# The RMS norm's work between two MLPs taken from two queues instead of one

## The chip, the cores and the metric

The kernel runs on one core of a Trainium2 chip. The metric is the device time of one execution in microseconds (us). The engines are named as the profile names them: PE (TensorE matmul) and PEld (its weight loads), DVE (VectorE), ACT (ScalarE), POOL (GpSimd), SP (SyncE, which here issues DMAs).

## The reference

Attention over 2 x 8 heads of 768 tokens with a band of 96 tokens, 8 global tokens and a linear distance bias, then two MLPs on the 1536 tokens of width 512, with an RMS norm between them:

```
attn_out = _attn_ref(q, k, v, n_global, n_local)
x = attn_out.transpose(0, 2, 1, 3).reshape(B * S, H * D)
h = x @ w_in                                  # 512 -> 2048
x = (h * tanh(log1p(exp(h)))) @ w_out         # 2048 -> 512
rms = sqrt(mean(x * x, axis=-1, keepdims=True) + 1e-06)
xn = x / rms * rms_g
g, val = xn @ w_gate, xn @ w_val              # 512 -> 1536 each
out = (g * sigmoid(g) * val) @ w_out2         # 1536 -> 512
```

All inputs and the output are float32.

## The kernel before

Every product is made of three matmuls: both factors are held as a high part, rounded to the matmul's type, and a low part, the rest (high x high, high x low, low x high). The weights arrive as float32 bits and are turned into the two parts on the way: a `Piece` is one 128 x 512 tile of weights, whose integer steps (L154 to L175) and low part (L194) run on DVE and whose high part runs on ACT (L190). The 1536 tokens stand in four blocks of 384 tokens.

The kernel has three stages, attention, the first MLP (`mlp1`, `mish1`) and the second (`mlp2`). The first MLP has 32 steps, eight to each quarter of the 2048 hidden columns: in step s PE makes the products of two chunks of 128 hidden columns for one block (`products`, L362, 24 matmuls of 384 columns) and then, through `flush`, the accumulation of the step before (`accumulate`, L414, 18 matmuls of 512 columns, into the three PSUM banks s0 to s2). ACT and DVE turn the products into the activation: tanh, arctan and sine on ACT (L382, L387, L388, with a load of ACT's table ahead of tanh and of arctan), a multiplication on DVE (L391), the high part on ACT (L488), the low part on DVE (L492). At the end of a step the next weight piece is begun (`begin`), two in every eighth step. After every second accumulation DVE adds the banks to the block's sums (L426). The second MLP has 48 steps of one chunk: 24 matmuls for gate and value, nine for the accumulation of the step before.

Between the two stands the norm of each block (`rms_norm`), which is queued when the block's last accumulation is recorded. It has three parts. `inverse`: three squares with a sum along the row on ACT (L459, whose unwanted output goes to PSUM bank s3), then two small instructions on POOL (L464, L467). `scale`: three multiplications of the sums on DVE (L471). `split_y`, four times: three transposes on PE into bank s3 (L442), a copy with the norm's gain on ACT that makes the high part (L446) and a subtraction on DVE that makes the low part (L447). The four results of a block are what its products in the second MLP read.

The order of the work on each engine is the order in which the program records it; there is no scheduler. The norm's parts stand in one list, `deferred`, five entries to a block: the inverse, the scaling with the first split, and three more splits. `do_deferred` takes one entry: once at the end of a step of the first MLP, and in a step of the second MLP once between the products and the accumulation and once behind the accumulation. A block's first step in the second MLP empties the list as far as it needs.

Of the kernel before, what the change touches and what calls it, by code (L numbers as in the profile page):

```python
# [22 lines left out]
NK = DM // P  # L23
# [27 lines left out]
def tile_attention_mish_swiglu(  # L51
# [31 lines left out]
    def nm(s):  # L83
        uid[0] += 1
        return f"{s}_{uid[0]}"

    def bank(tag, bufs=1):
        return psum.tile([P, BANK], F32, tag=tag, bufs=bufs, name=nm(tag))

    def mm_bank():  # L90
        return bank("mm", 4)
# [9 lines left out]
    order = []  # L101
# [20 lines left out]
    def conv_alloc(i):  # L122
        wpool = wearly if i % sum(SLOTS) < SLOTS[0] else late[0]
        W[order[i]] = wpool.tile([P, 2, WPIECE], F32R, tag="w", name=nm("w"))
# [212 lines left out]
    def fresh():  # L337

        for x in (W, staged, ys):
            x.clear()  # L340
        for x in (begun, pend, deferred, acc):
            del x[:]
        loaded[0], started[0] = 0, NW_EARLY
        for i in range(NW_EARLY):
            conv_alloc(i)
        for blk in range(NBLK):
            xs[blk] = [
                hl.tile([P, 2, BT], F32R, tag="hl", name=nm("hl")) for _ in range(NK)
            ]
# [7 lines left out]
    def products(ps, wkey, c, xs, kcs=tuple(range(NK))):  # L357
        col = slice((c % 4) * P, (c % 4 + 1) * P)
        for kc in kcs:
            w = W[wkey, kc, c // 4]  # L360
            for i, (wi, xi) in enumerate(((0, 0), (0, 1), (1, 0))):
                pe.matmul(  # L362
                    ps[:, 0:BT],
                    w[:, wi, col],
                    xs[kc][:, xi, :],
                    start=kc == 0 and i == 0,
                    stop=kc == NK - 1 and i == 2,
                )
# [25 lines left out]
    started = [NW_EARLY]  # L394
    begun = []

    def begin(n):
        for _ in range(n):
            begun.append(Piece(started[0]))
            begun[-1]("b3")  # L400
            started[0] += 1
# [4 lines left out]
    def accumulate(wkey, gt, c, blk, done):  # L406

        w = W[wkey, c]
        if c % 4 == 0:
            acc[:] = [bank(f"s{m}") for m in range(TB)]  # L410
        for m in range(TB):
            tok = slice(m * P, (m + 1) * P)
            for i, (gi, wi) in enumerate(((0, 0), (0, 1), (1, 0))):
                pe.matmul(  # L414
                    acc[m],
                    gt[:, gi, tok],
                    w[:, wi, :],
                    start=c % 4 == 0 and i == 0,
                    stop=c % 4 == 3 and i == 2,
                )  # L420
            if c % 4 == 3:
                if c == 3:
                    dve.tensor_copy(sums[blk][:, m, :], acc[m])
                else:
                    y = sums[blk][:, m, :]
                    dve.tensor_tensor(y, y, acc[m], op=ALU.add)  # L426
                done(m)

    acc = []
    ys = {}  # L430

    deferred = []

    def do_deferred():
        if deferred:
            deferred.pop(0)()

    def split_y(y, blk, kc):
        t = hl.tile([P, 2, BT], F32R, tag="hl", name=nm("hl"))
        tr = bank("s3")  # L440
        for m in range(TB):
            pe.transpose(  # L442
                tr[:, m * P : (m + 1) * P], y[:, m, kc * P : (kc + 1) * P], ident
            )
        g = gcol[:, kc : kc + 1]
        act.activation(t[:, 0, :], tr[:, 0:BT], AF.Copy, scale=g)  # L446
        dve.scalar_tensor_tensor(  # L447
            t[:, 1, :], tr[:, 0:BT], g, t[:, 0, :].bitcast(F32),
            op0=ALU.mult, op1=ALU.subtract,
        )  # L450
        ys.setdefault(blk, []).append(t)

    def rms_norm(blk):
        y = sums[blk]
        ss = cpool.tile([P, 2, TB], F32, tag="ss", name=nm("ss"), bufs=2)

        def square(m):
            junk = bank("s3")
            act.activation(junk, y[:, m, :], AF.Square, accum_out=ss[:, 0, m : m + 1])  # L459

        def inverse():
            for m in range(TB):
                square(m)
            pool.tensor_scalar(  # L464
                ss[:, 1, :], ss[:, 0, :], 1.0 / DM, 1.0e-6, op0=ALU.mult, op1=ALU.add
            )
            pool.tensor_tensor(ss[:, 0, :], ss[:, 1, :], mhalf, op=ALU.pow)  # L467

        def scale():
            for m in range(TB):  # L470
                dve.tensor_scalar(  # L471
                    y[:, m, :], y[:, m, :], ss[:, 0, m : m + 1], None, op0=ALU.mult
                )

        deferred.append(inverse)
        deferred.append(lambda: [scale(), split_y(y, blk, 0)])
        deferred.extend([lambda kc=kc: split_y(y, blk, kc) for kc in range(1, NK)])

    pend = []

    def flush(n):
        while len(pend) > n:
            pend.pop(0)()


    def split_hi(x):
        gt = gp.tile([P, 2, BT], F32R, tag="g", name=nm("g"))
        act.activation(gt[:, 0, :], x, AF.Copy)  # L488
        return gt

    def split_lo(gt, x):
        dve.tensor_tensor(gt[:, 1, :], x, gt[:, 0, :].bitcast(F32), op=ALU.subtract)  # L492

    def chunks(s):
        return [4 * (s // (2 * NBLK)) + 2 * (s % 2) + i for i in range(2)]

    def mish1(s, mish):

        blk, cs = s // 2 % NBLK, chunks(s)
        for i in range(2):  # L500
            mish.tanh(i)
        flush(0)
        mish.cosine()
        old = begun[:]
        del begun[:]
        for piece in old[:1]:
            piece("hi")
        for i in range(2):
            mish.times(i)
        for piece in old[:1]:  # L510
            piece("lo")
        gt = [split_hi(mish.t[:, i, :]) for i in range(2)]
        for piece in old[1:]:
            piece("hi")
        for i in range(2):
            split_lo(gt[i], mish.t[:, i, :])
        for piece in old[1:]:
            piece("lo")
        do_deferred()
        begin(BEGUN1[s])  # L520

        def later():
            def done(m):
                if m == TB - 1 and cs[1] == NC1 - 1:
                    rms_norm(blk)

            for c, g in zip(cs, gt):
                accumulate("out", g, c, blk, done)

        pend.append(later)  # L530

    def mlp1(s0):
        for s in range(s0, NC1 * NBLK // 2):
            banks = [mm_bank() for _ in range(2)]
            for ps, c in zip(banks, chunks(s)):
                products(ps, "in", c, xs[s // 2 % NBLK])
            mish1(s, Mish(banks))

    def mlp2():
        for s in range(NC2 * NBLK):  # L540
            blk = s // 4 % NBLK
            c = 4 * (s // (4 * NBLK)) + s % 4
            pg, pv = mm_bank(), mm_bank()
            if s % 4 == 0:
                while len(ys.get(blk, ())) < NK:
                    do_deferred()
            for kc in range(NK):
                products(pg, "gate", c, ys[blk], (kc,))
                products(pv, "val", c, ys[blk], (kc,))
            do_deferred()  # L550
            flush(0)
            do_deferred()
            r = dpool.tile([P, 2, BT], F32, tag="d", name=nm("r"))[:, 0, :]
            act.activation(r, pg[:, 0:BT], AF.Silu)  # L554
            dve.tensor_tensor(r, r, pv[:, 0:BT], op=ALU.mult)  # L555
            gt = split_hi(r)
            split_lo(gt, r)
            for piece in begun:
                piece.rest()
            del begun[:]  # L560
            begin(BEGUN2[s])

            def later(blk=blk, c=c, gt=gt):
                def done(m):
                    if c == NC2 - 1:
                        row = blk * BT + m * P
                        sp.dma_start(out[row : row + P, :], sums[blk][:, m, :])

                accumulate("out2", gt, c, blk, done)

            pend.append(later)
        flush(0)
        assert started[0] == len(order) and not begun and not deferred

    def mlps(s, mish=None):

# [10 lines left out]

    def attention_banded():
        fresh()
        mm = [mm_bank() for _ in range(4)]  # L590
        with ExitStack() as st:
# [211 lines left out]

    def attention_general():
        fresh()
        mm = [mm_bank() for _ in range(4)]
        with ExitStack() as st:
# [148 lines left out]
```

## Time and profile before

| | |
|---|---|
| median of 3 runs | 701.08 us (700.76 to 701.08) |
| the profiled execution | 700.8 us |
| its span, first to last instruction | 699.0 us |
| mean granted clock of TensorE | 0.989 |
| PE busy | 674.5 us, 96% of the span |
| PEld busy | 589.4 us, 84% |
| DVE, ACT, POOL busy | 451.1, 386.8, 70.2 us |

The attention fills about the first 110 us of the span (its first products of the first MLP are mixed into its end), the first MLP follows to about 371, the second to the end. A matmul's end is modelled, so a group of them is best measured from its start to the start of the next. The granted clock is 1.00 at the higher of PE's two levels, 2.4 GHz, and 0.50 at the lower, 1.2 GHz.

### The profile page before, as it was taken

Reading aid. Unit: us, or ns where it says so; the run is one execution under the profiler, and the core shown is the slowest. Engines: PE = TensorE matmul, PEld = TensorE weight load, DVE = VectorE, ACT = ScalarE, POOL = GpSimd, SP = SyncE. Lnnn points to the kernel's source line nnn. Section 1 sums busy time; section 2 is a strip of 40 time slices with the busy share of each in tenths; the row PEclk is TensorE's granted clock in tenths of the full one; section 3 lists DMA queues with packets and bytes.
Section 4 is the critical chain, followed back from the end, with each engine's and each line's share of the span. In section 5 each row is a group of like instructions: output and inputs, shape, how many; then the busy total and the mean of one; then the engine's idle time right before and its main releaser. Section 6 shows DMA issues by size and latency. Waiting matters only on the chain.

```text
span 699.0 us, 10036 instructions
## 1 busy us (share of the span) xinstructions
PE 674.5 (96%) x3760; PEld 589.4 (84%) x3760; DVE 451.1 (65%) x1067; ACT 386.8 (55%) x722; POOL 70.2 (10%) x128
## 2 busy tenths in 40 slices
PE   8999999999999999999898998999999999999997
PEld 3656668999999999998797886999999999999996
DVE  6787846887788778776885676874367775331332
ACT  5889869888888888888684542222113222111111
POOL 3667740000000000001001000000000000000000
PEclk9999999999999999999999998999999999999999
DMA  7977511231121113221112121131022100010111
GB/s 241 291 237 202 177 62 34 88 91 60 61 92 60 61 61 90 77 76 60 61 61 60 31 60 61 62 108 43 1 61 90 61 31 0 1 46 1 45 46 49
DMA packets 26728, 54.20 MB, mean 78 GB/s; under 512 B 2608, under 2 KB 14640, under 8 KB 26672
## 3 DMA queue, kind: packets, MB, share of 16 engines
q1 hardware_dynamic: 25968, 53.16, 23.9%
q8 instruction: 31, 0.51, 0.3%
q10 hardware_dynamic: 704, 0.33, 0.2%
q14 instruction: 25, 0.20, 0.1%
HBM read 50.34 MB, written 3.15 MB: 77 GB/s over the span
## 4 chain that ended last, share of the span: by engine, by line
PE 81%; DVE 8%; ACT 8%; issue 1%; POOL 1%; DMA 0%; DVEq 0%; SPq 0%; ACTq 0%; POOLq 0%
PE mm L362 43%; PE s L414 31%; PE mm L640 2%; PE s L725 2%; ACT e L671 2%; PE s L705 1%; DVE e L661 1%; ACT s L459 1%; DVE x L426 1%; PE s L442 1%; ACT g L488 1%; DVE hl L447 1%; DVE hl L353 1%; DVE bits L175 1%; ACT hl L352 1%
## 5 line engine op out<-in xcount | busy, mean ns | idle before, releaser
L362 PE MATMUL mm<-hl,w 128*128 128x384 f32 x1920 | 350.9, 337 | 0.0
L362 PEld LDWEIGHTS mm<-hl,w 128*128 128x128 f32 x1920 | 337.2, 188 | 6.7 <-issue 1.0
L414 PE MATMUL s<-w,g 128*128 128x512 f32 x1008 | 248.5, 396 | 0.0
L414 PEld LDWEIGHTS s<-w,g 128*128 128x128 f32 x1008 | 190.2, 190 | 36.8
L554 ACT ACTIVATE r<-mm 128x384 f32<-128x384 f32 x48 | 23.6, 491 | 141.1 <-PE mm L362 141.1
L555 DVE TENSOR_TENSOR r<-r,mm 128x384 f32<-128x384 f32 x48 | 26.4, 550 | 69.2 <-ACT r L554 69.2
L426 DVE TENSOR_TENSOR x<-x,s 128x512 f32<-128x512 f32 x60 | 40.8, 687 | 46.1 <-PE s L414 46.1
L488 ACT ACTIVATE g<-r 128x384 fp32r<-128x384 f32 x48 | 25.2, 526 | 65.6 <-DVE r L555 65.6
L391 DVE TENSOR_TENSOR d<-d,mm 128x384 f32<-128x384 f32 x64 | 32.5, 549 | 40.4 <-ACT d L388 40.4
L690 POOL TENSOR_SCALAR e<-e,s 128x256 f32<-128x256 f32 (+1 forms) x96 | 47.9, 513 | 35.0 <-DVE bias L621 10.2
L671 ACT ACTIVATE e<-e,s 128x256 f32<-128x256 f32 (+1 forms) x96 | 46.1, 481 | 7.9 <-DVE s L661 7.6
L169 DVE SCALAR_TENSOR_TENSOR bits<-stage,bits 128x512 int32<-128x512 int32 x68 | 48.2, 708 | 2.1
L175 DVE SCALAR_TENSOR_TENSOR bits<-stage,bits 128x512 int32<-128x512 int32 x68 | 47.2, 694 | 2.0
L492 DVE TENSOR_TENSOR g<-r,g 128x384 fp32r<-128x384 f32 x48 | 26.8, 558 | 28.4 <-ACT g L488 28.4
L488 ACT ACTIVATE g<-d 128x384 fp32r<-128x384 f32 x64 | 33.5, 526 | 19.3 <-DVE d L391 17.7
L382 ACT ACTIVATE d<-mm 128x384 f32<-128x384 f32 x64 | 30.8, 492 | 20.8 <-PE mm L362 19.2
L386 ACT ACT_TABLE_LOAD x32 | 41.1, 1283 | 0.6
L194 DVE TENSOR_TENSOR w<-bits,w 128x512 fp32r<-128x512 f32 x60 | 41.3, 688 | 0.0
L382 ACT ACT_TABLE_LOAD x31 | 39.8, 1283 | 0.6
L190 ACT ACTIVATE w<-bits 128x512 fp32r<-128x512 f32 x60 | 37.0, 616 | 0.0
L640 PE MATMUL mm<-k,q 64*128 64x256 f32 (+1 forms) x168 | 31.9, 410 | 4.5 <-DVE s L661 2.6
L661 DVE CUSTOM_DVE_ANT_0 e<-mm,bias 128x256 f32<-128x256 f32 (+1 forms) x96 | 35.0, 396 | 0.6 <-POOL e L690 0.6
(82 smaller groups left out, 510.4 us busy)
## 6 DMA issues: line engine op xcount, KB each, us to landing
stage<-in_w_out_dram SPq DMA_DIRECT2D x28, 512.0 KB, 3.2
stage<-in_w_in_dram SPq DMA_DIRECT2D x16, 512.0 KB, 3.9
stage<-in_w_gate_dram SPq DMA_DIRECT2D x12, 512.0 KB, 3.4
stage<-in_w_val_dram SPq DMA_DIRECT2D x12, 512.0 KB, 3.5
k<-in_kT_dram SPq DMA_DIRECT2D x7, 704.0 KB, 4.2
out_dram<-x SPq DMA_DIRECT2D x12, 256.0 KB, 2.1
q<-in_qT_dram SPq DMA_DIRECT2D x7, 384.0 KB, 5.1
v<-in_v_dram SPq DMA_DIRECT2D x7, 384.0 KB, 6.2
```

The source lines that it names most:

```text
L169: dve.scalar_tensor_tensor(self.bits, self.lw, 29, self.bits, op0=ALU.logical_shift_right, op1=ALU.bitwise_or,)
L175: dve.scalar_tensor_tensor(self.bits, self.hw, -1073741824, self.bits, op0=ALU.bitwise_and, op1=ALU.bitwise_or,)
L194: engine.tensor_tensor(self.wt[:, 1, :], self.fl, self.wt[:, 0, :].bitcast(F32), op=ALU.subtract)
L362: pe.matmul(ps[:, 0:BT], w[:, wi, col], xs[kc][:, xi, :], start=kc == 0 and i == 0, stop=kc == NK - 1 and i == 2,)
L382: act.activation(self.t[:, i, :], self.h[i], AF.Tanh, scale=0.5)
L414: pe.matmul(acc[m], gt[:, gi, tok], w[:, wi, :], start=c % 4 == 0 and i == 0, stop=c % 4 == 3 and i == 2,)
L426: dve.tensor_tensor(y, y, acc[m], op=ALU.add)
L488: act.activation(gt[:, 0, :], x, AF.Copy)
L640: pe.matmul(banks[j][:, 0 : n * P], qs[b, p][r, t * P : (t + 1) * P], ks[b, p][r, 0, :] if t == 0 else ks[b, p][r, t : t + NT : NT - 1, :] ...
L661: dve.tensor_tensor_reduce(e[:, j, 0:n], banks[j][:, 0:n], bias0[:, h, :] if t == 0 else bias[:, h, :], scale=-0.125, scalar=3.0e38, op0=A ...
L671: act.activation(e[:, j, 0:n], e[:, j, 0:n], AF.Exp, scale=-1.0, bias=s[:, 0, j : j + 1], accum_out=s[:, 1, j : j + 1],)
L690: pool.tensor_scalar(e[:, j, 0:n], e[:, j, 0:n], s[:, 3, j : j + 1], 0.0, op0=ALU.mult, op1=ALU.add,)
```

## The change

The list `deferred` becomes two. `ends` holds the inverse and the scaling of each block; one entry is taken at the end of a step, in both MLPs. `between` holds the four splits; they are put there when the scaling is recorded, and one is taken in a step of either MLP between the products and the accumulation. In the first MLP that place is behind the tanh, ahead of `flush`. A step of the second MLP thus records one split where it recorded up to two, and a block's scaling and its first split are no longer in one entry.

```diff
@@ -338,7 +338,7 @@
 
         for x in (W, staged, ys):
             x.clear()
-        for x in (begun, pend, deferred, acc):
+        for x in (begun, pend, between, ends, acc):
             del x[:]
         loaded[0], started[0] = 0, NW_EARLY
         for i in range(NW_EARLY):
@@ -429,11 +429,12 @@
     acc = []
     ys = {}
 
-    deferred = []
-
-    def do_deferred():
-        if deferred:
-            deferred.pop(0)()
+
+    between, ends = [], []
+
+    def do_one(work):
+        if work:
+            work.pop(0)()
 
     def split_y(y, blk, kc):
         t = hl.tile([P, 2, BT], F32R, tag="hl", name=nm("hl"))
@@ -471,10 +472,9 @@
                 dve.tensor_scalar(
                     y[:, m, :], y[:, m, :], ss[:, 0, m : m + 1], None, op0=ALU.mult
                 )
-
-        deferred.append(inverse)
-        deferred.append(lambda: [scale(), split_y(y, blk, 0)])
-        deferred.extend([lambda kc=kc: split_y(y, blk, kc) for kc in range(1, NK)])
+            between.extend([lambda kc=kc: split_y(y, blk, kc) for kc in range(NK)])
+
+        ends.extend([inverse, scale])
 
     pend = []
 
@@ -499,6 +499,7 @@
         blk, cs = s // 2 % NBLK, chunks(s)
         for i in range(2):
             mish.tanh(i)
+        do_one(between)
         flush(0)
         mish.cosine()
         old = begun[:]
@@ -516,7 +517,7 @@
             split_lo(gt[i], mish.t[:, i, :])
         for piece in old[1:]:
             piece("lo")
-        do_deferred()
+        do_one(ends)
         begin(BEGUN1[s])
 
         def later():
@@ -541,15 +542,12 @@
             blk = s // 4 % NBLK
             c = 4 * (s // (4 * NBLK)) + s % 4
             pg, pv = mm_bank(), mm_bank()
-            if s % 4 == 0:
-                while len(ys.get(blk, ())) < NK:
-                    do_deferred()
+            assert len(ys[blk]) == NK
             for kc in range(NK):
                 products(pg, "gate", c, ys[blk], (kc,))
                 products(pv, "val", c, ys[blk], (kc,))
-            do_deferred()
+            do_one(between)
             flush(0)
-            do_deferred()
             r = dpool.tile([P, 2, BT], F32, tag="d", name=nm("r"))[:, 0, :]
             act.activation(r, pg[:, 0:BT], AF.Silu)
             dve.tensor_tensor(r, r, pv[:, 0:BT], op=ALU.mult)
@@ -557,6 +555,7 @@
             split_lo(gt, r)
             for piece in begun:
                 piece.rest()
+            do_one(ends)
             del begun[:]
             begin(BEGUN2[s])
 
@@ -570,7 +569,7 @@
 
             pend.append(later)
         flush(0)
-        assert started[0] == len(order) and not begun and not deferred
+        assert started[0] == len(order) and not begun and not between and not ends
 
     def mlps(s, mish=None):
 
```

PE, around the step in which the first block's first set of transposes stands (`ident,x`; mm is a bank of products, s an accumulation or bank s3). Before:

```order
L414 MATMUL s_561_3545<-w_3052,g_3495 128x512 x3
L414 MATMUL s_562_3546<-w_3052,g_3495 128x512 x3
L442 MATMUL s_567_3583<-ident,x_84 128x128 [waits DVE_49,PE_49,Activation_49]
L442 MATMUL s_567_3583<-ident,x_84 128x128 [waits DVE_49] x2
L362 MATMUL mm_3605<-hl_182,w_2684 128x384 x3
L362 MATMUL mm_3605<-hl_183,w_2756 128x384 x3
```

Now:

```order
L362 MATMUL mm_3599<-hl_184,w_2828 128x384 x3
L362 MATMUL mm_3599<-hl_185,w_2900 128x384 x3
L443 MATMUL s_574_3628<-ident,x_84 128x128 [waits DVE_49,PE_49,Activation_49]
L443 MATMUL s_574_3628<-ident,x_84 128x128 [waits DVE_49] x2
L414 MATMUL s_560_3544<-w_3061,g_3573 128x512 [waits Activation_49]
L414 MATMUL s_560_3544<-w_3061,g_3573 128x512 x2
```

The set stood behind an accumulation and ahead of the product block; now it stands behind that product block and ahead of the next accumulation.

ACT and PE, at the second set of the same block. ACT before, from the high parts of one step (`g`) to the tanh of the next (`d<-mm`), the split's copy being `hl<-s`:

```order
L488 ACTIVATE g_3664<-d_3631 128x384 [waits DVE_49]
L488 ACTIVATE g_3666<-d_3631 128x384 [waits DVE_49,PE_49]
L190 ACTIVATE w_3668<-bits_3597 128x512
L446 ACTIVATE hl_3673<-s_581_3674,small 128x384 [waits PE_49]
L382 ACT_TABLE_LOAD
L382 ACTIVATE d_3714<-mm_3688 128x384 [waits PE_49]
```

ACT now, where `s,ss<-x` are the squares of the second block:

```order
L190 ACTIVATE w_3668<-bits_3590 128x512
L460 ACTIVATE s_580_3673,ss_3655<-x_85 128x512
L460 ACTIVATE s_581_3675,ss_3655<-x_85 128x512 [waits Activation_49]
L460 ACTIVATE s_582_3677,ss_3655<-x_85 128x512 [waits Activation_49]
L382 ACT_TABLE_LOAD
L382 ACTIVATE d_3715<-mm_3689 128x384 [waits PE_49]
L382 ACTIVATE d_3715<-mm_3690 128x384 [waits PE_49]
L447 ACTIVATE hl_3718<-s_589_3719,small 128x384 [waits PE_49]
```

And the second set on PE, now:

```order
L362 MATMUL mm_3690<-hl_184,w_2828 128x384 x3
L362 MATMUL mm_3690<-hl_185,w_2900 128x384 x3
L443 MATMUL s_589_3719<-ident,x_84 128x128 [waits DVE_49,Activation_49]
L443 MATMUL s_589_3719<-ident,x_84 128x128 x2
L414 MATMUL s_590_3725<-w_2972,g_3664 128x512 [waits DVE_49]
```

The squares of the second block came behind all four sets of the first; now they stand between its first and its second set, and the second set has a wait for ACT.

DVE, from the first scaling on (`x<-x,ss`; `bits` are the integer steps of two weight pieces, `hl<-s` the split's subtraction). Before:

```order
L471 TENSOR_SCALAR x_84<-x_84,ss_3484 128x512 x3
L447 SCALAR_TENSOR_TENSOR hl_3582<-s_567_3583,small,hl_3582 128x384
L154 TENSOR_SCALAR bits_3589<-stage_3360 128x512
L160 TENSOR_SCALAR bits_3589<-bits_3589 128x512
L163 TENSOR_SCALAR bits_3589<-bits_3589 128x512
```

Now:

```order
L169 SCALAR_TENSOR_TENSOR bits_3590<-stage_3432,bits_3590 128x512 [waits DVE_49]
L175 SCALAR_TENSOR_TENSOR bits_3590<-stage_3432,bits_3590 128x512 [waits DVE_49]
L448 SCALAR_TENSOR_TENSOR hl_3627<-s_574_3628,small,hl_3627 128x384 [waits Activation_49]
L426 TENSOR_TENSOR x_85<-x_85,s_560_3544 128x512 [waits PE_49]
L426 TENSOR_TENSOR x_85<-x_85,s_561_3545 128x512 [waits PE_49]
```

The subtraction came right behind the scaling, ahead of the two pieces' ten instructions; now it stands behind them and right ahead of the additions of the next accumulation.

## Rows read from the trace of the kernel before

**Rows 1.** Waits, 305 to 445 us: engine and line waited for: us, times, longest.

```profile
PE s L442 <- DVE x L471: 11.8, 4, 4.6
...
PE s L442 <- DVE hl L447: 0.5, 2, 0.3
```

**Rows 2.** Timeline of PE, 300 to 476 us: start, us, line, idle before in brackets.

```profile
322.06 4.35 PE L362 MATMUL mm<-hl,w 128*128 128x384 f32 x24
326.24 4.28 PE L414 MATMUL s<-w,g 128*128 128x512 f32 x18
335.15 1.18 PE L442 MATMUL s<-ident,x 128*128 128x128 f32 x3 [4.63 <-DVE x L471]
335.98 5.57 PE L362 MATMUL mm<-hl,w 128*128 128x384 f32 x24
341.39 4.29 PE L414 MATMUL s<-w,g 128*128 128x512 f32 x18
345.51 0.49 PE L442 MATMUL s<-ident,x 128*128 128x128 f32 x3
...
350.01 4.29 PE L414 MATMUL s<-w,g 128*128 128x512 f32 x18
...
377.90 1.03 PE L442 MATMUL s<-ident,x 128*128 128x128 f32 x3 [2.13 <-DVE x L471]
378.69 5.98 PE L414 MATMUL s<-w,g 128*128 128x512 f32 x18
...
398.88 1.03 PE L442 MATMUL s<-ident,x 128*128 128x128 f32 x3 [0.69 <-DVE x L471]
...
422.42 1.18 PE L442 MATMUL s<-ident,x 128*128 128x128 f32 x3 [4.38 <-DVE x L471]
...
441.20 4.35 PE L362 MATMUL mm<-hl,w 128*128 128x384 f32 x24
...
447.47 4.35 PE L362 MATMUL mm<-hl,w 128*128 128x384 f32 x24
```

**Rows 3.** Stretches: length, busy of PE, PEld, DVE, ACT, POOL, granted clock, DMA.

```profile
399.66:403.94 4.28, 4.28 (x26) 4.24 (x27) 2.76 (x6) 2.01 (x4) 0.00 (x0) 1.00 0.17 70
335.98:338.70 2.72, 2.72 (x10) 2.72 (x11) 1.65 (x4) 1.86 (x2) 0.00 (x0) 0.54 0.00 0
...
423.25:425.20 1.95, 1.95 (x6) 1.56 (x7) 0.62 (x1) 0.58 (x1) 0.00 (x0) 0.50 0.65 231
```

**Rows 4.** Timeline of DVE, 305 to 385 us, around the first scaling.

```profile
334.52 1.27 DVE L471 TENSOR_SCALAR x<-x,ss 128x512 f32<-128x512 f32 x3
336.98 0.62 DVE L447 SCALAR_TENSOR_TENSOR hl<-s,small,hl 128x384 fp32r<-128x384 f32 x1 [1.18 <-ACT hl L446]
337.51 0.42 DVE L154 TENSOR_SCALAR bits<-stage 128x512 int32<-128x512 int32 x1
...
342.33 0.69 DVE L175 SCALAR_TENSOR_TENSOR bits<-stage,bits 128x512 int32<-128x512 int32 x1
344.35 2.05 DVE L426 TENSOR_TENSOR x<-x,s 128x512 f32<-128x512 f32 x3 [1.33 <-PE s L414]
```

**Rows 5.** Timeline of ACT, 305 to 385 us, two steps of the first MLP.

```profile
318.13 0.49 ACT L382 ACTIVATE d<-mm 128x384 f32<-128x384 f32 x1 [1.12 <-PE mm L362]
...
324.40 0.58 ACT L459 ACTIVATE s<-x 128x512 f32<-128x512 f32 x1
...
326.64 1.28 ACT L382 ACT_TABLE_LOAD   x1
...
346.90 1.05 ACT L488 ACTIVATE g<-d 128x384 fp32r<-128x384 f32 x2 [1.08 <-DVE d L391]
...
348.37 0.56 ACT L446 ACTIVATE hl<-s,small 128x384 fp32r<-128x384 f32 x1
```

## The prediction

> **What bounds the kernel now.** I read the waits of TensorE (PE) first, then PE's own timeline around them, then the granted clock of those stretches, and last VectorE (DVE) and ScalarE (ACT) around the first of them. In the waits almost nothing is left that holds PE in the two MLP stages, except the transposes of L442: they waited 11.8 us in four waits for the scaling of L471 and 0.5 us for the subtraction of L447 [rows 1]. In PE's timeline the reader is to see the pitch of undisturbed work and then the holes. A block of 24 products takes 4.18 us (322.06 to 326.24), 18 accumulations take 4.12 (341.39 to 345.51), transposes and products together 4.50 (345.51 to 350.01), so one set of three transposes costs 0.32; a step of the second MLP is 6.27 long (441.20 to 447.47), so its nine accumulations take 2.09 [rows 2]. The holes stand in brackets: 4.63 us before the first block's set at 335.15, 2.13 at 377.90, 0.69 at 398.88, 4.38 at 422.42 [rows 2].
>
> The holes cost more than their length. The product block behind the first took 5.41 us (335.98 to 341.39) instead of 4.18, and the 18 accumulations behind the second lasted 5.98 where such a group else lasts 4.29 [rows 2]; the granted clock there was 0.54 and 0.50, the lower of the two levels (1.2 and 2.4 GHz), after PE had stood idle. After the hole of 0.69 it stayed at 1.00 [rows 2, 3]. So I take the whole price from one difference: from 322.06 to 441.20 PE needed 119.14 us. In it lie 13 product blocks, 6 accumulations of the first MLP, 7 of the second and 16 sets of transposes: 13 x 4.18 + 6 x 4.12 + 7 x 2.09 + 16 x 0.32 = 98.8 us. **The norm's holes and the slow clock behind them cost 20.3 us** [rows 2]; that is the ceiling of what the change can give back.
>
> **The change, part by part.** No instruction is added or removed; all are moved, none of them a DMA. The loads are issued from the weight conversion, whose place in the steps stays, so SP's queue keeps its order; POOL keeps its two instructions behind the squares and has nothing else there. A step here is a product block, the sets that follow it, and the accumulation of the step before.
>
> First set. Nothing ahead of it changes but its place on PE, so the scaling starts at 334.52 as now [rows 4] and the set runs at 335.15 to 335.98, one transpose per scaled third, as now [rows 2]. But the product block that stood behind it now runs in the hole: it starts when the accumulation of 326.24 ends, at 330.36, and ends at 334.54. What is left is a wait of 0.6 us and 0.83 instead of 0.32 for the set: 1.1 us. This is the cover that the move buys, 4.18 us of products; where the scaling is more than that late, the rest still shows.
>
> The later sets of each block. They need no new scaling. But they need their bank. All sets and all squares use the one bank s3, and the squares of the next block are now recorded at the end of a step, the next set after the product block behind it. In the changed order the second set therefore waits for ACT, which it does not now. When do those squares end? On DVE two weight pieces were begun in this step, and the subtraction of the first set is now queued behind both: the scaling ends at 334.52 + 1.27 = 335.8, the pieces take 5.5 (337.51 to 342.33 + 0.69), the subtraction 0.53 (336.98 to 337.51), the three additions of the accumulation 2.05: 343.85 [rows 4]. The accumulation itself is over at 340.1, so DVE is what is late. ACT's rounding copies start about 0.5 us behind such additions (344.35 + 2.05 = 346.40 on DVE, 346.90 on ACT), and it comes to the end of its step 1.47 later (346.90 to 348.37) [rows 4, 5]: 345.8. Three squares take 2.24 (324.40 to 326.64) [rows 5]: 348.05. The second set is due at 335.98 + 4.12 + 4.18 = 344.28. **That is a new wait of about 3.8 us plus the hand-over; I take 3.9**, with 3.5 and 4.5 as its ends. Who waits for that: the set's accumulation on PE, ACT's next copy, and behind it the whole next step.
>
> The clock behind it. A wait of 3.9 us lies between 2.13 and 4.63, after both of which PE's clock fell, at 1.2 us (5.41 - 4.18) and 1.7 us (5.98 - 4.29) [rows 2, 3]. I take 1.5.
>
> Squares twice more meet a set in the next step: those of the third block the fourth set, those of the last block a set early in the second MLP. No row shows this. From below: a step of ACT with squares takes 8.51 us now (318.13 to 326.64); with the copy of 0.56 that now stands in it, 9.07 [rows 5]; the next set is due 8.62 after (4.12 + 4.18 + 0.32) [rows 2], so the wait is at least 0.45. From above: where DVE's subtraction (0.53) and scaling (1.27) stand in front of its additions [rows 4], 1.8 more, 2.2. I take 1.0 for each, nearer the lower end since in these steps only one piece is begun. After holes of that size the clock is between two rows (0.69 stayed, 2.13 fell); I take it as staying, and keep 1.7 each for the range.
>
> The other sets, and the scaling and squares of the second MLP, I cost at nothing: a step there gives ACT and DVE 6.27 us. If that cover went, each would show by its own length, 1.1 us for an evacuation.
>
> Sum: 1.1 + 3.9 + 1.5 + 2 x 1.0 = 8.5 us of holes stay or are new; 20.3 - 8.5 = 11.8 us are won. The profiled execution took 700.8 us, so 689.0; the median of the runs is 0.28 above it, so **689.3 us**.
>
> **A rule weighed against the rows.** The two short waits for L447 came where one set followed another within a step, 0.5 us in sum, and no row shows a set that is held by the set of a whole step before [rows 1]. The Trainium skill, "Perfetto Trace Analysis", section Matmuls (under Optimizing Tensor Performance), says that independent groups should rotate through different PSUM banks, so that the evacuation of one overlaps the next; here sixteen sets and all squares share one bank. By the rows the sets a step apart cost nothing, which gives 689.3; by the rule each would show its evacuation, which is the second rival.
>
> **The rivals.** (1) The clock falls three times and the short waits are at their upper end: 1.1 + 4.5 + 1.7 + 2 x (2.2 + 1.7) = 15.1, so 5.2 won, 695.9. For it: the wait of 2.13 was enough. Against: two of the three waits are half as long.
> (2) Slower: one bank for everything. It is the mechanism of the rule above, priced from rows alone. Every set waits until the set before it is evacuated, 0.56 copy and 0.53 subtraction, on PE's path; 15 sets x 1.1 = 16.4 on top of 8.5, 24.9 against 20.3: 4.6 slower, 705.7. It decides where a subtraction ends later than the next set is due. For it: the subtraction now stands behind the weight pieces on DVE. Against: even behind two pieces it ends at 341.8, and the next set is due at 344.28.
> (3) The squares are in time, and the bank holds nothing: only the 1.1 stays, 19.2 won, 681.9. For it: in 20.3 us of earlier holes ACT had room. Against: in the profile a step of ACT with squares is already 8.51 long and gets a copy more.
> (4) The change does not do what it says, sets or scaling standing where they stood: 701. The order of the changed program speaks against it.
>
> **How the numbers follow.** Forecast 0.67, rival 1 0.20, rival 2 0.05, rival 3 0.06, rival 4 or anything else within 0.2% 0.02. The range goes from a wait of 3.5 with none of the short ones and no slow clock (4.6 of holes, 15.7 won: 685.4) to rival 1 (696.0); rivals 2 and 3, 4, and a few per cent of the rest lie outside, some 0.18. 0.2% is 1.4 us, about what a measurement of this kernel can tell from no change: faster 0.93, same 0.02, slower 0.05.
>
> **What would show it.** Right: PE's waits for L471 shrink from 11.8 to about 1.5 us, in one place; a new row of PE waiting for ACT's squares (L460 in the changed file) with some 6 us in three waits, the longest near 344 us and close to 4; the clock at 1.00 in the second MLP, and one fall near 348. Wrong: no wait for the squares (rival 3); waits for the subtraction, L448, at many sets (rival 2); a product stage that no longer keeps 4.18 per block away from the holes, which would make the ceiling itself wrong.

## The result, and the profile after

The changed kernel takes 689.93 us, the median of six runs (688.42 to 691.27), against 701.08 before: a ratio of 0.9838, 95% interval 0.9823 to 0.9853. The forecast was 689.3, the range 685.4 to 696.0. The profiled execution took 688.42 us against 700.8, its span is 686.6 us against 699.0, the mean granted clock 0.997 against 0.989; PE is busy 669.5 us, 98% of the span.

PE's waits between 300 and 455 us in the changed kernel (engine and line waited for: us, times, longest):

```profile
PE s L443 <- ACT s L460: 4.4, 3, 3.3
PE s L443 <- DVE x L472: 0.4, 1, 0.4
```

The 11.8 us for the scaling and the 0.5 us for the subtraction [rows 1] are gone but for 0.4 us. In their place stands a wait that the kernel before did not have, for the squares: 4.4 us in three places, 3.3 us the longest.

PE's timeline (start, us, engine, line, operation; the idle time before a row in brackets), the rows that answer to [rows 2]:

```profile
322.03 4.35 PE L362 MATMUL mm<-hl,w 128*128 128x384 f32 x24
...
330.33 4.35 PE L362 MATMUL mm<-hl,w 128*128 128x384 f32 x24
335.13 1.03 PE L443 MATMUL s<-ident,x 128*128 128x128 f32 x3 [0.45 <-DVE x L472]
335.91 4.38 PE L414 MATMUL s<-w,g 128*128 128x512 f32 x18
340.13 4.35 PE L362 MATMUL mm<-hl,w 128*128 128x384 f32 x24
347.76 0.55 PE L443 MATMUL s<-ident,x 128*128 128x128 f32 x3 [3.29 <-ACT s L460]
348.07 5.99 PE L414 MATMUL s<-w,g 128*128 128x512 f32 x18
353.89 4.36 PE L362 MATMUL mm<-hl,w 128*128 128x384 f32 x24
358.08 0.49 PE L443 MATMUL s<-ident,x 128*128 128x128 f32 x3
...
362.53 4.35 PE L362 MATMUL mm<-hl,w 128*128 128x384 f32 x24
367.14 0.55 PE L443 MATMUL s<-ident,x 128*128 128x128 f32 x3 [0.26 <-ACT s L460]
...
385.50 0.55 PE L443 MATMUL s<-ident,x 128*128 128x128 f32 x3 [0.86 <-ACT s L460]
```

The product block of 330.33 now lies where the kernel before stood idle; the first set still runs at 335.13, as at 335.15 [rows 2], since the scaling that it waits for has not moved, and 0.45 us is left of a wait of 4.63. The second set comes 3.45 us behind the end of its product block (340.13 + 4.18 = 344.31), the fourth 0.4 late at 367.14, the second block's second set 1.0 late at 385.50. All other sets follow their products at once, like that of 358.08; from there to the next products are 4.45 us, a set and 18 accumulations without a wait.

The accumulations behind the long wait lasted 5.99 us. The clock there and behind the short wait of 367.14 (length, busy of the engines, granted clock, DMA):

```profile
347.76:350.00 2.24, 2.24 (x9) 1.85 (x10) 1.48 (x3) 2.23 (x4) 1.41 (x2) 0.69 0.00 0
350.00:353.89 3.89, 3.89 (x15) 3.07 (x13) 0.89 (x2) 3.83 (x5) 0.00 (x0) 0.74 0.41 135
367.44:371.65 4.21, 4.21 (x21) 3.47 (x20) 1.77 (x3) 4.17 (x6) 1.16 (x1) 1.00 0.44 125
```

DVE and ACT ahead of the second set, beside [rows 4, 5]:

```profile
334.50 1.27 DVE L472 TENSOR_SCALAR x<-x,ss 128x512 f32<-128x512 f32 x3
335.69 0.42 DVE L154 TENSOR_SCALAR bits<-stage 128x512 int32<-128x512 int32 x1
...
340.51 0.69 DVE L175 SCALAR_TENSOR_TENSOR bits<-stage,bits 128x512 int32<-128x512 int32 x1
341.12 0.61 DVE L448 SCALAR_TENSOR_TENSOR hl<-s,small,hl 128x384 fp32r<-128x384 f32 x1
341.65 1.87 DVE L426 TENSOR_TENSOR x<-x,s 128x512 f32<-128x512 f32 x3
```

```profile
344.02 1.05 ACT L488 ACTIVATE g<-d 128x384 fp32r<-128x384 f32 x2 [3.50 <-DVE d L391]
344.97 0.61 ACT L190 ACTIVATE w<-bits 128x512 fp32r<-128x512 f32 x1
345.49 0.58 ACT L460 ACTIVATE s<-x 128x512 f32<-128x512 f32 x1
...
347.73 1.28 ACT L382 ACT_TABLE_LOAD   x1
```

The reader can follow the forecast chain row by row: the scaling at 334.50; two weight pieces from 335.69 to the last instruction at 340.51; the subtraction behind them at 341.12 (336.98 before); the additions from 341.65, though the accumulation that they add was over at 340.1; ACT's rounding copies at 344.02; the high part of the second of the two weight pieces at 344.97; the squares from 345.49; and the table load at 347.73, at which moment PE takes up the set (347.76).

### The profile page after: what moved, and what is told of

Same layout as the page of the kernel before. It is cut to its first block, busy times and chain, and to the rows that moved or that the text cites. A ratio compares the mean times of both kernels' runs of the same rounds, so it can differ in the third digit from the quotient of the medians.

```text
span 686.6 us, 10023 instructions
## 1 busy us (share of the span) xinstructions
PE 669.5 (98%) x3760; PEld 587.1 (86%) x3760; DVE 450.2 (66%) x1067; ACT 385.9 (56%) x722; POOL 68.2 (10%) x128
## 4 chain that ended last, share of the span: by engine, by line
PE 84%; ACT 7%; DVE 6%; DMA 1%; issue 1%; SPq 0%; DVEq 0%
PE mm L362 45%; PE s L414 31%; PE mm L639 2%; PE s L724 2%; ACT e L670 2%; PE s L704 2%; DVE x L426 1%; ACT s L460 1%; DVE e L660 1%; DMA q<-in_qT_dram 1%; PE mm L273 1%; PE s L443 1%; DVE hl L353 1%; ACT hl L352 1%; PE mm L647 1%
```

## The experiments

To compare traces apart from the start and the end of a run, which vary (last section), I use the stretch from the product block ahead of that of 330.33 to the last 18 accumulations of the program. Ahead of it PE's order is the same in all. Before, it goes from 322.06 [rows 2] to 689.79, 367.7 us; in the changed kernel from 322.03 to 677.44, 355.4: 12.3 won.

| kernel | median, us | ratio to before, 95% interval | from, us | to, us | length, us | won there, us |
|---|---|---|---|---|---|---|
| change | 689.93 | 0.9838 (0.9823 to 0.9853) | 322.03 | 677.44 | 355.4 | 12.3 |
| squares to SBUF | 686.74 | 0.9784 (0.9760 to 0.9808) | 322.49 | 674.42 | 351.9 | 15.8 |
| pieces earlier | 686.22 | 0.9784 (0.9762 to 0.9807) | 323.36 | 674.72 | 351.4 | 16.4 |
| sets at the end | 694.03 | 0.9878 (0.9854 to 0.9902) | 324.86 | 682.96 | 358.1 | 9.6 |
| scaling joined | 696.01 | 0.9913 (0.9890 to 0.9936) | 323.70 | 684.59 | 360.9 | 6.8 |
| both of the first two | 683.02 | 0.9717 (0.9700 to 0.9734) | 323.87 | 672.78 | 348.9 | 18.8 |
| change again | 690.87 | 0.9849 (0.9825 to 0.9873) | 323.90 | 678.27 | 354.4 | 13.4 |

The kernel before took 702.09 us beside the first four experiments and 702.41 beside the last two. Each length in the table is that of one execution; the two of the change differ by 1.0 us.

The theory: the separation of scaling and sets, and the product block between them, give back most of the 20.3 us; what is not given back is the second set, held by the squares of the next block through the one bank s3, and the squares are late because the subtraction and the additions stand behind two weight pieces on DVE. The rivals: ACT's own chain is the bound and the bank only where it shows; or one half of the change alone, the place or the separation, gives the gain.

**The bank.** The squares' unwanted output goes to SBUF:

```diff
-            junk = bank("s3")
+            junk = cpool.tile([P, DM], BF16, tag="junk", name=nm("junk"))
```

> The squares write their unwanted output to SBUF, so that the transposes no longer share bank s3 with them. Theory (the bank holds the set): PE's waits for the squares, 4.4 us in the changed kernel's trace, and the slow clock behind the longest (1.7 us) go; ACT is still late, so the accumulations behind the first and second sets wait for ACT's high parts, some 3 us in sum. 685 to 687 us, no wait of PE for L460. Rival (ACT's lateness itself is the bound, the bank only where it shows): the same 6 us come back as waits of the accumulations (L414) for L488 and L492: 689 to 690.

686.74 us. PE's timeline, from three of the sets to the products behind their accumulations:

```profile
344.78 0.49 PE L443 MATMUL s<-ident,x 128*128 128x128 f32 x3
...
349.80 4.35 PE L362 MATMUL mm<-hl,w 128*128 128x384 f32 x24
353.99 0.49 PE L443 MATMUL s<-ident,x 128*128 128x128 f32 x3
355.25 0.73 PE L414 MATMUL s<-w,g 128*128 128x512 f32 x2 [0.77 <-ACT g L488]
356.24 3.91 PE L414 MATMUL s<-w,g 128*128 128x512 f32 x16 [0.25 <-DVE g L492]
359.99 4.35 PE L362 MATMUL mm<-hl,w 128*128 128x384 f32 x24
...
372.86 0.49 PE L443 MATMUL s<-ident,x 128*128 128x128 f32 x3
...
378.35 4.35 PE L362 MATMUL mm<-hl,w 128*128 128x384 f32 x24
```

No set waits for the squares. But where a set and its 18 accumulations take 4.45 us undisturbed, they take 5.02, 6.00 and 5.49 here, 3.2 us more in sum, where 3 were expected. The granted clock stayed at 1.00; PE's waits in these accumulations for ACT's high parts and DVE's low parts come to 1.0 and 0.7 us as the profile counts them, and the rest shows only in the pitch. Of the 6.5 us that the bank cost in the changed kernel's trace (waits of 3.45, 0.4 and 1.0, and 1.6 of slow clock) 3.5 are won, 15.8 against 12.3. So the bank was what held the set, as the theory has it; the rival is right for about half: behind the bank ACT's lateness comes to light. Whether that lateness is ACT's own, the next edit and the one with both show.

**The two pieces on DVE.** The step with two weight pieces is moved from the fourth of eight to the first:

```diff
-BEGUN1 = [1 + (s % 8 == 3) for s in range(NC1 * NBLK // 2)]
+BEGUN1 = [1 + (s % 8 == 0) for s in range(NC1 * NBLK // 2)]
```

> The step of eight in which two weight pieces are begun is the first and no longer the fourth, so that only one piece stands on DVE between the first scaling and the subtraction of the first set. Theory (DVE's two pieces make the squares late, and with them the second set): the wait of 3.3 us at the second set shrinks by the 2.7 us of one piece to under 1, and the clock does not fall there: 4.4 us less, 684 to 686.5. Rival (the hole is that of ACT's own chain with a copy and three squares more): it stays over 2.5 us, time within 1 us of 690.

686.22 us. The three sets that wait, in PE's timeline:

```profile
346.08 0.55 PE L443 MATMUL s<-ident,x 128*128 128x128 f32 x3 [0.27 <-ACT s L460]
...
364.44 0.55 PE L443 MATMUL s<-ident,x 128*128 128x128 f32 x3 [0.87 <-ACT s L460]
...
382.80 0.55 PE L443 MATMUL s<-ident,x 128*128 128x128 f32 x3 [0.86 <-ACT s L460]
```

ACT ahead of the second set:

```profile
342.85 1.05 ACT L488 ACTIVATE g<-d 128x384 fp32r<-128x384 f32 x2 [0.98 <-DVE d L391]
343.81 0.58 ACT L460 ACTIVATE s<-x 128x512 f32<-128x512 f32 x1
```

At the second set the wait is 0.27 us, 3.0 less than in the change; two pieces are 5.4 us of DVE (335.69 to 341.12 in the changed kernel), so one is 2.7. The other two sets wait 0.87 and 0.86 us, where the change had 0.26 and 0.86. This edit leaves the bank and the order of the norm's parts as they are, so it is the second piece that made the squares late. Most of that came through DVE, but not all: the piece's high part on ACT, 0.61 us at 344.97 in the change, is gone from in front of the squares too, which now follow the rounding copies by 0.96 us (342.85 to 343.81) and not by 1.47 (344.02 to 345.49). So about 2.5 of the 3.0 us came through DVE and 0.5 through ACT. 4.1 us more are won than by the change, which is about the 3.0 of the wait and the 1.6 of slow clock behind it, less the 0.6 by which the fourth set waits longer.

**The place alone undone.** Two queues, but the sets stand at the end of a step, ahead of the other queue's entry:

```diff
             mish.tanh(i)
-        do_one(between)
...
+        do_one(between)
         do_one(ends)
...
-            do_one(between)
             flush(0)
...
+            do_one(between)
             do_one(ends)
```

> Two queues as in the change, but a set is recorded at the end of a step, ahead of the entry of the other queue, where the old queue stood, and not between products and accumulation. Theory (the place counts too): PE waits no longer for the scaling nor much for the squares, but accumulations wait for ACT's high parts (about 3.5 us in sum, since products no longer stand ahead of a set), and the first products of the second MLP wait for the first block's fourth set, which stands right ahead of them: 4 to 5 us at L362 with a slow clock behind it. 691 to 693. Rival (only the separation of scaling and sets counts): 690 or less, and with the bank free of squares down to 684.

694.03 us. PE's timeline, the places where it waited:

```profile
358.30 0.73 PE L414 MATMUL s<-w,g 128*128 128x512 f32 x2 [1.83 <-ACT g L488]
359.28 5.51 PE L414 MATMUL s<-w,g 128*128 128x512 f32 x16 [0.25 <-DVE g L492]
...
378.83 0.44 PE L362 MATMUL mm<-hl,w 128*128 128x384 f32 x1 [1.93 <-ACT hl L447]
379.81 1.87 PE L362 MATMUL mm<-hl,w 128*128 128x384 f32 x5 [0.55 <-DVE hl L448]
381.48 5.18 PE L414 MATMUL s<-w,g 128*128 128x512 f32 x18
```

With the sets at the end of a step and the scaling an entry of its own, the first set stands a step later than in the kernel before. No set waits for the scaling or the squares. But the accumulations wait 2.6 us for ACT and 0.5 for DVE, where 3.5 were expected, 1.83 the longest, and the first products of the second MLP wait 1.93 and 0.55 us for the results of the fourth set, which stands right ahead of them; behind both the clock is slow (16 accumulations in 5.51 us, 18 in 5.18). I had expected 4 to 5 us at the products; it was 2.5. The median lies 1 us over the upper end of the expectation; why is not shown. The profiled run (695.09 us) had lost 2.8 us ahead of the compared stretch (324.86). The rival is out: separation without the place gives 9.6 of the 12.3 us.

**The separation alone undone.** The scaling is recorded with the first set again, at the new place:

```diff
-            between.extend([lambda kc=kc: split_y(y, blk, kc) for kc in range(NK)])
-        ends.extend([inverse, scale])
+        def inverse_then_splits():
+            inverse()
+            between.append(lambda: [scale(), split_y(y, blk, 0)])
+            between.extend([lambda kc=kc: split_y(y, blk, kc) for kc in range(1, NK)])
+        ends.append(inverse_then_splits)
```

> Sets between products and accumulation as in the change, but the scaling is recorded with the first set of its block again, right ahead of it. Theory (the separation counts): PE waits for L472 at four places again, some 3.4, 2.5, 0.7 and 0.7 us, two of them with a slow clock behind, and for squares twice: 8 us of the 20 come back less, 695 to 698. Rival (the place alone gives the gain): 690 or less, waits for L472 under 2 us in sum.

696.01 us. PE's waits, 300 to 460 us, and the two longest in its timeline:

```profile
PE s L443 <- DVE x L472: 6.4, 4, 3.1
PE s L443 <- ACT s L460: 1.0, 2, 0.8
```

```profile
331.18 1.17 PE L443 MATMUL s<-ident,x 128*128 128x128 f32 x3 [3.12 <-DVE x L472]
332.00 6.88 PE L414 MATMUL s<-w,g 128*128 128x512 f32 x18
...
372.27 1.03 PE L443 MATMUL s<-ident,x 128*128 128x128 f32 x3 [2.26 <-DVE x L472]
373.06 4.37 PE L414 MATMUL s<-w,g 128*128 128x512 f32 x18
```

The four waits for the scaling are back, 6.4 us where 7.3 were expected, and two for the squares. The joined entry also brings the first set a step earlier than in the change, behind the product block of 323.70 with which the stretch begins; that is what joining them means here, since the set no longer comes a step behind its scaling. The place without the separation gives 6.8 us. Either half alone thus gives part of the 12.3, the separation more than the place, and 9.6 and 6.8 together are more than the whole: they cover the same holes in part. Behind the first wait the accumulations take 6.88 us instead of some 4.3; behind 2.26 they take 4.37, no fall of the clock, where two had been expected.

**Both repairs.** The first two edits together:

> Both of the first two edits: squares to SBUF, two pieces begun in the first step of eight. Theory: of the holes only that of the first scaling (1.1 us) and up to 1 us of waits for ACT and DVE at accumulations stay, and the clock does not fall: 18 us less than before, some 3 us less than either edit alone, a ratio of 0.973 to 0.976. Rival (ACT is late whatever the bank and the pieces): no better than either edit alone, 0.978, with the waits at L414.

683.02 us, 19.4 less than the 702.41 before, where 18 were expected; the ratio of 0.9717 lies just below the range of 0.973 to 0.976. All that is left of PE's waits between 300 and 460 us:

```profile
PE s L443 <- DVE x L472: 0.4, 1, 0.4
```

18.8 of the 20.3 us are won; the 1.1 us of the first set, which the forecast had as the part that this order cannot cover, is nearly all that stays. The rival is out: ACT's lateness, which the SBUF run alone had laid bare, went with the second piece, and only one group of 18 accumulations, at 372.31, takes 0.2 us longer than the others. This version beats both kernels; its interval lies clear of the change's and of those of either edit alone.

**The change again**, beside the last one:

> The changed kernel unaltered, beside the last one on the same chip: 0.982 to 0.985 of before, with the same three waits for the squares, 3.3, 0.3 and 0.9 us, and the same fall of the clock behind the longest. If the fall is not there in this run, the time is about 1.5 us less and the hole alone is the cost.

690.87 us. PE's timeline, the sets that wait and the accumulation behind the longest wait:

```profile
337.00 1.03 PE L443 MATMUL s<-ident,x 128*128 128x128 f32 x3 [0.44 <-DVE x L472]
...
349.63 0.55 PE L443 MATMUL s<-ident,x 128*128 128x128 f32 x3 [3.28 <-ACT s L460]
349.93 4.37 PE L414 MATMUL s<-w,g 128*128 128x512 f32 x18
...
367.99 0.55 PE L443 MATMUL s<-ident,x 128*128 128x128 f32 x3 [0.86 <-ACT s L460]
...
386.34 0.55 PE L443 MATMUL s<-ident,x 128*128 128x128 f32 x3 [0.88 <-ACT s L460]
```

The long wait is the same, 3.28 us. But the accumulations behind it took 4.37 us and not 5.99: the clock did not fall. The fourth set then waited 0.86 us, where 0.3 had been expected and the first run had 0.26: from the second set to the products ahead of the fourth PE took 1.6 us less than in the first run (349.63 to 362.77 against 347.76 to 362.53), ACT from squares to squares only 1.0 less (the table loads behind them stand at 349.59 and 367.95 against 347.73 and 367.10). So this fall cost 1.6 us on the spot and 1.0 over the stretch (355.4 against 354.4). The execution as a whole was not shorter, as had been expected for a run without the fall, but longer, 690.73 against 688.42 us: it lost 1.9 us ahead of the stretch and 1.4 behind it.

## Why the prediction was right, point by point

**The ceiling, 20.3 us.** Measured through the pitch of undisturbed work it holds: the version with both repairs wins 18.8 and has 1.1 left at the first set. PE's waits alone, 12.3 us [rows 1], would have put the ceiling at what the change itself won, with 8 us of holes still in it.

**The first set, 1.1 us.** From 330.33 to the accumulation at 335.91 are 5.58 us; a product block and a set are 4.50: 1.08.

**The second set, 3.9 us.** It was 3.45, just under the lower end of 3.5. Every time in the chain came within 0.4 us of the forecast; the largest single difference is that the three additions took 1.87 us and not 2.05, and the squares began at 345.5 and not 345.8. (The forecast's own terms give 343.88 for the end of the additions, where it writes 343.85.) The experiment on the bank shows what held the set, and the one on the pieces what made the squares late: mostly DVE, as forecast, and with 0.5 us the piece's copy on ACT, which the forecast has inside its 1.47.

**The clock behind it, 1.5 us.** 5.99 against 4.37 for the same group at the full clock, 1.6, in the profiled run; none in the other profiled run of the same kernel. The step was right as a size and wrong as a certainty, and that the first run had the fall was in part luck. The clocks of 0.54 and 0.50 that the prediction reads for the first hole and the second are those of the first and the fourth [rows 3]; behind the second it was 0.64 (378.69 to 381.50). The prices were taken from the lengths and do not rest on this.

**The two short waits, 1.0 each.** They cost 0.4 and 1.0; in the run without the fall 1.0 each, with waits of 0.86 and 0.88. No row had shown them; the lower bound of 0.45 lies at the one measured and the upper of 2.2 far off. That 1.0, a choice between the two, came out so closely is in part luck. The clock stayed up behind them, as taken.

**The sum.** 1.1 + 3.45 + 1.6 + 0.4 + 1.0 = 7.6 of the 8.5 that the forecast left standing; 12.3 won in the compared stretch against 11.8, so 8.0 of the 20.3 stayed and 0.4 has no place in this list. The median moved by 11.1 us, and the forecast median was 0.6 us off; that is closer than the start and the end of a run allow (last section), so the path is borne out and the last half microsecond is luck. Of the signs, the waits for the scaling came to 0.4 us where 1.5 was said (the forecast's own term for the wait is 0.6), and those for the squares to 4.4 where 6 was said, in the places named.

**The rivals.** The clock fell once, not three times (rival 1). No set waited for the evacuation of the set before it: the subtraction behind two pieces ended at 341.65, 2.7 us ahead of the time the next set was due (rival 2); the one bank cost what it cost through the squares alone. The rule of the Trainium skill that stood beside it ("Perfetto Trace Analysis", section Matmuls) thus has no price in the changed kernel, where the sets stand 6.6 us or more apart. Before, where a set came 2.4 to 2.8 us behind another, two (406.74 and 434.57) waited 0.24 and 0.26 us for the subtraction of the one before, and one (391.41) did not. What held the second set in the changed kernel is no evacuation but a scratch output in the same bank, which the rule does not name. The squares were not in time (rival 3), and their freedom is worth what the SBUF run shows, less than rival 3 had, since ACT is late behind it. The sets and the scaling moved as the edit says (rival 4).

## What to carry to other kernels

Price a hole on the busiest engine by the pitch of the same work elsewhere, not by its idle row: here the waits said 12.3 us and 20.3 were to be had. When work is moved into another engine's gap, write down what then stands next in every in-order queue and in every single buffer: the sets found their place on PE, and a scratch output that nobody reads, in the same bank, held one of them for 3.3 us and two more for up to 0.9. An output that is thrown away belongs where nobody waits for it, and a step that carries extra work should not also be the one that starts two pieces of something else.

## What the runs showed of the hardware

The clock does not follow from the length of a hole alone. It fell with waits of 4.63, 2.13 and 4.38 us before [rows 2, 3], of 3.29 in the change and of 3.12 with the scaling joined, but stayed up with 3.28 in the change's other run and with 2.26 with the scaling joined; in the run with the sets at the end 1.83 followed by 0.25 was enough, and so was 1.93 followed by 0.55 (all by the length of the work behind the wait). A price for it is a chance times a size.

The start of a run is not the same in all: the block with which the compared stretch begins came between 322.0 and 324.9 us, with the same order ahead of it on PE. The first 30 us of three runs, the change, the change again and the sets at the end:

```profile
0.00:30.00 30.00, 25.75 (x178) 13.93 (x178) 21.02 (x119) 21.20 (x70) 13.18 (x32) 1.00 0.87 274
```

```profile
0.00:30.00 30.00, 25.50 (x162) 13.81 (x163) 19.06 (x110) 19.50 (x63) 12.02 (x30) 0.94 0.82 256
```

```profile
0.00:30.00 30.00, 25.36 (x161) 13.93 (x161) 18.12 (x105) 19.02 (x62) 11.03 (x29) 0.89 0.79 242
```

The granted clock there was 1.00, 0.94 and 0.89, and the block came at 322.03, 323.90 and 324.86. The end varies too: from the last 18 accumulations to the end of the span it is 9.2 us in the change (677.44 to 686.6) and 10.6 in its other run (678.27 to 688.9). That is as much as a small change is worth, which is why the traces above are compared between the two.
